# Moving the wait for the output store from in front of a block's closing barrier to behind it

## The chip, the cores and the metric

The kernel runs on one core of one Trainium2 chip. The metric is device time in microseconds (us). A core has five engines with an instruction stream each: TensorE (PE), VectorE (DVE), ScalarE (ACT), GpSimd (POOL) and SyncE (SP, which here issues nearly all DMAs). In this program they meet through semaphores: counters that an engine or a DMA adds to and that another engine waits on.

Everything here happens in the last four microseconds of a 658 us program.

## The reference

One decode step: layer norm of one token, grouped-query attention over a cache of 65,536 keys (32 query heads, 8 key-value heads of 128), the output projection, a GELU feed-forward beside it, and the residual.

```python
xn = _layernorm(x)
# A: q = xn @ wq; scores = q k^T / sqrt(128); p = softmax(scores); o = p v; o @ wo
# B: gelu(xn @ w1 + b1) @ w2 + b2
return x + A(xn, k_cache, v_cache, wq, wo) + B(xn, w1, b1, w2, b2)   # (1, 1, 512), bf16
```

## The kernel before

A small scheduler records each engine's operations with the semaphore waits that they need, and they are then emitted, engine by engine, inside one block. The end of the kernel is the only part that the change touches:

```python
# ... the last matmuls of the output projection write pR on PE ...
sch.op(DVE, lambda: dve.tensor_copy(out=fin_bf[0:NR, :], in_=pR[0:NR, 0:128]),      # L820
       reads=[f"pss{R}"], writes=["fin"])
ev_out = sch.dma(                                                                    # L824
    SP,
    lambda: sp.dma_start(out=out[0, 0].rearrange("(kt p) -> kt p", p=128), in_=fin_bf[0:NR:32, :]),
    sem_out, reads=["fin"], writes=["out_dram"],
)
sch.wait_ev(SP, ev_out)        # SyncE waits until the 1 KB result has landed

with nc.Block() as block:                                                            # L829
    # ... one function for each engine emits that engine's recorded operations ...
    @block.sync
    def _(e):
        _emit(e, SP.ops)
    # ...
# nothing follows
```

A block ends in a barrier of all engines. In the program as built it is this (shortened; every engine first branches into this common piece, and its Drain is the instruction with which it reports to the barrier):

```
ACT, PE, DVE, SP:  Drain, adds 1 to "gather";  then wait for "release", take 1 off it
POOL:              Drain;  wait until gather is 4, take 4 off;  add 4 to "release"
```

## Time and profile before

| | before |
|---|---|
| median time | 658.44 us (6 runs, 658.15 to 658.76) |
| span of the kernel's own instructions | 656.5 us |
| from the store's issue to its landing | 1.64 us |
| from the landing to the kernel's last instruction | 0.39 us |

First the page of the kernel before: its DMA row over 40 slices of the span (tenths of busy time), the load queue, and the chain that ended last.

```profile
DMA  8999999999999999999999999999999999999997
...
q1 hardware_dynamic: 8616, 280.50, 99.2%
...
DMA 63%; PE 34%; issue 2%; DVE 0%; SPq 0%
```

The kernel is a stream of the caches through the DMA engines; nothing in the change can touch that. So the reader has to look at the tail. These are three lines of the waits view of the kernel before, for SyncE's queue: source line, releaser, then total, count and longest wait in us.

```profile
SPq L824 <- DVE fin_bf L820: 16.6, 1, 16.6
SPq L829 <- DMA out_dram<-fin_bf: 1.0, 1, 1.0
SPq L829 <- PEq L829: 0.2, 1, 0.2
```

SyncE waits for VectorE's last copy, issues the store, then waits 1.0 us for the landing, and only then reaches the barrier, where it waits 0.2 us more. Now the instructions of line L829, the closing barrier of the kernel before. These are eight of the view's eleven lines, put in order of start; left out are SyncE, ACT and DVE passing at 656.5. Each line gives engine and operation, count, duration in ns (least, median, most), and the start in us.

```profile
L829 ACTq DRAIN  x1: 746/746/746, 643.0 to 643.0; - x1
L829 POOLq DRAIN  x1: 164/164/164, 643.9 to 643.9; - x1
L829 PEldq DRAIN  x1: 425/425/425, 653.8 to 653.8; - x1
L829 DVEq DRAIN  x1: 330/330/330, 654.2 to 654.2; - x1
L829 SPq COMPARE_BRANCH  x1: 33/33/33, 656.2 to 656.2; - x1
L829 SPq DRAIN  x1: 7/7/7, 656.3 to 656.3; - x1
L829 POOLq EVENT_SEMAPHORE  x2: 17/17/17, 656.4 to 656.4; - x2
L829 PEldq EVENT_SEMAPHORE  x1: 51/51/51, 656.5 to 656.5; - x1
```

Four engines have drained by 654.5 and then stand still for two microseconds. SyncE, held by its wait for the store (the wait sits on its branch), comes last, at 656.3.

The span ends with the kernel's own last instruction, but the program does not. The trace also records every semaphore update, and in these records activity goes on for 1.9 us behind the span. No view of the profile prints them; they are read from the packed trace. The Trainium skill, "Runtime: NRT & Kernel Launch", section "The ~15µs preamble/postamble breakdown", says what this is: behind the kernel the runtime puts a barrier over all engines, then a reset of the user semaphores, then another barrier. For the runtime's barrier in front of a kernel it describes a serpentine over the five engines in eight hops. It reserves semaphore 2 for that barrier (section "Semaphores 0–2 are reserved"). The records agree (nine updates make eight hops); in us from the store's issue, for the kernel before:

```
landing 1.64 | barrier released 1.95 | kernel's last instruction ends 2.03
semaphore 2, first pass : 2.264 2.298 2.505 2.549 2.572 2.677 2.716 2.751 2.797
other semaphores reset  : up to 3.36
semaphore 2, second pass: nine more updates, the last at 3.941
```

I call the first nine updates the closing chain, and the time from the store's issue to the last update of semaphore 2 the *tail*. It is 3.94 us before. That last update stands 658.46 us behind the start of the span, close to the time measured (658.33 us in the profiled run).

### The profile page before, as it was taken

To read this page: it belongs to the slowest core of one execution; us is meant where nothing else is said; L and a number is where in the kernel's file an instruction comes from. 1 tells how busy PE (TensorE), PEld (TensorE's weight loads), DVE (VectorE), ACT (ScalarE), POOL (GpSimd) and SP (SyncE) were. 2 spreads that over 40 slices of the span, in tenths; PEclk is the share of its full clock that TensorE was granted. 3 is DMA by queue.
4 is the path that set the end of the run, shared out by engine and by line. 5 is a ranking of instruction groups with operands and counts; after the bars stand their busy time and mean duration, and the time that the engine had idled before them with its cause. 6 is when DMAs were issued, how large, how long until landed. Compare 5 with 4: busy or idle time off the path is not lost.

```text
span 656.5 us, 27968 instructions
## 1 busy us (share of the span) xinstructions
PE 539.3 (82%) x12682; PEld 512.1 (78%) x12682; DVE 275.7 (42%) x574; ACT 244.9 (37%) x454; POOL 2.9 (0%) x27
## 2 busy tenths in 40 slices
PE   2388699999789797878969787896978879797897
PEld 0187698988689697868969786896968779686896
DVE  3244162635435172442616245171634516254353
ACT  0134153534425152351605335161443516144251
POOL 0000000000000000000000000000000000000000
PEclk9788597878759596885959778596877859687595
DMA  8999999999999999999999999999999999999997
GB/s 369 438 436 426 429 430 433 439 425 461 401 441 439 421 453 413 437 427 445 433 417 449 417 445 421 427 457 411 447 419 447 429 419 441 423 459 408 431 433 295
DMA packets 8774, 280.65 MB, mean 427 GB/s; under 512 B 1082, under 2 KB 1596, under 8 KB 1724
## 3 DMA queue, kind: packets, MB, share of 16 engines
q1 hardware_dynamic: 8616, 280.50, 99.2%
q8 instruction: 8, 0.13, 0.1%
q10 hardware_dynamic: 148, 0.01, 0.0%
q14 instruction: 2, 0.02, 0.0%
HBM read 280.50 MB, written 0.00 MB: 427 GB/s over the span
## 4 chain that ended last, share of the span: by engine, by line
DMA 63%; PE 34%; issue 2%; DVE 0%; SPq 0%
DMA kv<-in_A_k_cache_dram 61%; PE pst L590 27%; PE pss L610 4%; DMA kv<-in_A_wo_dram 3%; PE pO L681 2%; PE pA L637 0%; PE pA L648 0%; DVE pmax L618 0%; PE pA L697 0%; PE pss L805 0%; DVE gmax L639 0%; DVE diag L641 0%; SPq L470 0%; SPq L467 0%; SPq L463 0%
## 5 line engine op out<-in xcount | busy, mean ns | idle before, releaser
L590 PE MATMUL pst<-ident_bf,kv 128*128 128x128 bf16 x4096 | 284.3, 236 | 34.0 <-DMA kv<-in_A_k_cache_dram 33.9
L600 ACT ACTIVATE kt_ring<-pst 128x1024 bf16<-128x1024 bf16 x192 | 195.6, 1027 | 312.1 <-PE pst L590 310.7
L590 PEld LDWEIGHTS pst<-ident_bf,kv 128*128 128x128 bf16 x4096 | 266.0, 107 | 42.4 <-DMA kv<-in_A_k_cache_dram 35.5
L598 DVE COPY kt_ring<-pst 128x1024 bf16<-128x1024 bf16 x320 | 210.7, 687 | 121.1 <-PE pst L590 118.7
L681 PE MATMUL pO<-P_bf,kv 128*128 128x4 bf16 x4096 | 115.1, 166 | 37.1 <-DMA kv<-in_A_v_cache_dram 32.1
L681 PEld LDWEIGHTS pO<-P_bf,kv 128*128 128x128 bf16 x4096 | 113.6, 104 | 38.5 <-DMA kv<-in_A_v_cache_dram 33.1
L610 PE MATMUL pss<-q_cur,kt_ring 128*128 128x4 bf16 x4096 | 111.9, 164 | 4.9 <-issue 4.9
L610 PEld LDWEIGHTS pss<-q_cur,kt_ring 128*128 128x128 bf16 x4096 | 109.3, 96 | 5.1 <-issue 5.1
L659 ACT ACTIVATE P_bf<-pss,negm 128x128 bf16<-128x128 f32 x128 | 50.9, 547 | 67.6 <-DVE negm L651 67.6
L690 DVE COPY o_all<-pO 128x4 f32 (+1 forms) x32 | 5.2, 161 | 120.3 <-PE pO L681 119.5
L618 DVE TENSOR_REDUCE pmax<-pss 128x4 f32<-128x512 f32 x32 | 22.1, 691 | 68.8 <-PE pss L610 68.8
L659 ACT ACTIVATION_READ_ACCUMULATOR P_bf<-pss,negm 128x1 f32 x128 | 35.3, 276 | 0.0
L648 PEld LDWEIGHTS pA<-diag,ones_f 4*128 4x128 f32 x64 | 12.6, 245 | 17.8 <-DVE diag L641 16.2
L637 PE MATMUL pA<-ident_f,pmax 128*4 128x128 f32 x64 | 14.0, 305 | 12.5 <-DVE pmax L618 12.5
L648 PE MATMUL pA<-diag,ones_f 4*128 4x4 f32 x64 | 15.4, 309 | 10.0 <-DVE diag L641 10.0
L637 PEld LDWEIGHTS pA<-ident_f,pmax 128*4 128x4 f32 x64 | 2.9, 84 | 15.7 <-DVE pmax L618 14.0
L639 DVE TENSOR_REDUCE gmax<-pA 4x1 f32<-4x128 f32 x32 | 8.8, 274 | 9.1 <-PE pA L637 9.1
L673 DVE COPY sums_all<-sums 128x8 f32 (+1 forms) x16 | 2.7, 171 | 23.4 <-ACT P_bf L659 23.4
L697 PE MATMUL pA<-sums_all,ones_f 128*128 128x128 f32 x32 | 12.4, 491 | 0.0
L651 DVE TENSOR_SCALAR negm<-pA 128x4 f32<-128x4 f32 x32 | 5.1, 161 | 10.8 <-PE pA L648 10.8
L697 PEld LDWEIGHTS pA<-sums_all,ones_f 128*128 128x128 f32 x32 | 8.1, 312 | 0.0
L641 DVE TENSOR_SCALAR diag<-ident_f,gmax 4x4 f32<-4x4 f32 x32 | 7.0, 218 | 1.1
(78 smaller groups left out, 49.5 us busy)
## 6 DMA issues: line engine op xcount, KB each, us to landing
kv<-in_A_k_cache_dram SPq DMA_DIRECT2D x32, 4096.0 KB, 27.5
kv<-in_A_v_cache_dram SPq DMA_DIRECT2D x4, 4096.0 KB, 23.2
kv<-in_A_wq_dram SPq DMA_DIRECT2D x1, 4096.0 KB, 12.2
kv<-in_B_w_dram SPq DMA_DIRECT2D x2, 1792.0 KB, 18.0
kv<-in_A_wo_dram SPq DMA_DIRECT2D x1, 2048.0 KB, 23.0
kv<-in_A_wo_dram SPq DMA_DIRECT2D x1, 1024.0 KB, 25.1
kv<-in_A_wo_dram SPq DMA_DIRECT2D x1, 512.0 KB, 25.9
kv<-in_A_wo_dram SPq DMA_DIRECT2D x1, 384.0 KB, 16.4
```

What stands on the lines that cost most here:

```text
L590: lambda tb=tb, at=at, b=b, tt=s * TPB + t: pe.transpose(pst[tb][:, at * 128:(at + 1) * 128], slot[b][:, tt, :], ident_bf[:, :]),
L598: e, fn = DVE, lambda tb=tb, dst=dst: dve.tensor_copy(out=dst, in_=pst[tb][:, :])
L600: e, fn = ACT, lambda tb=tb, dst=dst: act.activation(out=dst, in_=pst[tb][:, :], func=ACTF.Copy)
L610: lambda k=k, kb=kb, at=at, t=t: pe.matmul(pss[k][:, at:at + HPG], lhsT=kt_ring[:, kb * BCOL + t * 128:kb * BCOL + (t + 1) * 128], rhs=q_c ...
L618: lambda k=k: dve.tensor_reduce(out=pmax[:, :], in_=pss[k][:, 0:CW].rearrange("p (t j) -> p j t", j=HPG), axis=AX.X, op=ALU.max),
L637: sch.op(PE, lambda: pe.matmul(pA[0:HPG, PA_ST:PA_ST + 128], lhsT=pmax[:, 0:HPG], rhs=ident_f[:, :], start=True, stop=True), reads=["pmax" ...
L639: sch.op(DVE, lambda: dve.tensor_reduce(out=gmax4[:, :], in_=pA[0:HPG, PA_ST:PA_ST + 128], axis=AX.X, op=ALU.max), reads=["pA"], writes=[" ...
L641: sch.op(DVE, lambda: dve.tensor_scalar(out=diag4[:, :], in0=ident_f[0:HPG, 0:HPG], scalar1=gmax4[0:HPG, 0:1], scalar2=None, op0=ALU.mult) ...
L648: sch.op(PE, lambda: pe.matmul(pA[:, PA_SB:PA_SB + HPG], lhsT=ones_f[0:HPG, 0:128], rhs=diag4[0:HPG, 0:HPG], start=True, stop=True), reads ...
L659: lambda k=k, at=at, j=j, src=src: act.activation(out=P_v[k][:, :, j], in_=src[:, :, j], func=ACTF.Exp, bias=negm[:, at:at + 1], scale=1.0 ...
L681: lambda k=k, t=t: pe.matmul(pO[:, 0:HPG], lhsT=vslot[:, k * TPD + t, :], rhs=P_v[k][:, t, :], start=t == 0, stop=t == TPD - 1),
L697: sch.op(PE, lambda: pe.matmul(pA[:, PA_SUM:PA_SUM + NC], lhsT=ones_f[:, :], rhs=sums_all[:, :], start=True, stop=True), reads=["ones_f", ...
```

## The change

SyncE still waits for the store, but as its own last instruction, behind the barrier. The output has still landed before the program ends, because the runtime's closing barrier needs SyncE too (experiments 2 and 4 show it waiting for SyncE).

```diff
         sem_out, reads=["fin"], writes=["out_dram"],
     )
-    sch.wait_ev(SP, ev_out)
 
     with nc.Block() as block:
@@
         @block.tensor
         def _(e):
             _emit_rolled(e, PE.ops, marks)
+
+    sp.wait_ge(ev_out.sem, ev_out.val)
```

The intent is that the engines pass the barrier while the store is still on its way.

## The prediction

> **What bounds the kernel now.** It streams the key and value caches. The page's slices show the 16 DMA engines busy at nine tenths in 38 of 40 slices, the load queue at 99.2% of the span, 427 GB/s; the chain that ended last is 63% DMA and 34% PE. The span is 656.5 us, the timed median 658.46 us. The change touches none of that: the instruction order of PE, DVE, ACT and POOL is the same in both programs, and SyncE differs only behind the output store.
>
> **The tail of before** (trace records at the end of the span; the waits view of SyncE's queue agrees: 1.0, 0.2 us):
> - 654.52: the store is issued, 0.63 us, until 655.15.
> - 656.15: its semaphore is full. SyncE waits 1.0 us for it in its branch (starts 656.17, 33 ns).
> - 656.33: SyncE's drain, 0.12 us after the branch, the last arrival at the barrier. The others drained earlier: PE 653.8, DVE 654.2, ACT and POOL near 643 to 644.
> - 656.36 and 656.44: POOL gathers and releases; 656.48 to 656.49: four engines pass; PE ends last at 656.54.
>
> So branch, drain, gather and release cost 656.54 - 656.15 = 0.39 us in series behind the landing.
>
> **What the change does.** It moves that stretch into the shadow of the landing. SyncE branches at about 655.15 and drains by 655.35, the engines pass near 655.5, and SyncE alone waits for the landing, about 0.6 us more. It adds one SyncE wait (17 to 33 ns). It removes no transfer and not the landing time. The Trainium skill, "DMA: Bandwidth & Descriptors", section on the anatomy of one DMA, puts about 2 us of fixed cost on a transfer, mostly the write receipt; here issue to landing is 656.15 - 654.52 = 1.63 us, packets moving at 655.75 to 655.81. That stays, because SyncE must still end behind it.
>
> **Behind the span.** The Trainium skill, "Runtime: NRT & Kernel Launch", launch sequence, says a closing barrier over all engines and semaphore resets follow the kernel. The trace agrees: updates of semaphore 2 run from 656.78 to 657.31 in one chain, resets of the others to 657.88, a second chain from 658.10 to 658.46. In the first chain the third step came 0.21 us after the second, in the second chain 0.04 us: an engine arrived late. Now SyncE alone will be late. If it stands first in that chain, the 0.17 us hole goes too; if later, it is its own gain only. I can't tell which.
>
> **Sum** (estimate). Span: 656.54 to about 656.19, -0.35 us. Timed: -0.32 to -0.5 us, say -0.4 us. All of it is on the critical path, being the end of the program, but it is 0.06% of the time, and the three runs of before spread over 0.6 us (658.15 to 658.76).
>
> **Predicted: 658.05 us, range 657.6 to 658.5.** Faster by over 2%: 0.003; within 2%: 0.994; slower: 0.003.
>
> **What would show each step.**
> - Right: barrier events of ACT, DVE, PE, POOL near 655.4 to 655.6, before the store's landing; the span's last instruction is SyncE's wait, 20 to 50 ns after the landing; span about 0.35 us shorter measured from the store's issue; issue to landing still 1.5 to 1.8 us; the first chain of semaphore 2 begins sooner after the landing, or waits in the middle for SyncE.
> - Wrong: the barrier finishing behind the landing; a longer issue to landing; the closing chain no sooner.
>
> **What would make it wrong.** Run noise is as large as the effect, so the median may move either way. SyncE's drain may wait for the outstanding store: then nothing is hidden. The landing time may vary by some tenths. The timed interval may begin or end elsewhere than I read it.

## The result, and the profile after

The changed kernel takes 657.60 us (median of 6 runs, 657.51 to 657.80) against 658.44 us (658.15 to 658.76). The ratio is 0.9988, with a 95% interval of 0.9975 to 1.0001. Ratios here are the mean time of one kernel's runs over that of the other's of the same rounds, so they are not quite the ratio of the medians. The interval just includes 1. Yet over the whole study the 16 runs of the changed kernel lie between 657.48 and 658.03 us and 33 runs of the kernel before between 658.14 and 658.76 us, so they don't overlap. The means of the three sessions differ by 0.78, 0.68 and 0.76 us. The sign of the gain is not in doubt.

The page after, for the same three lines:

```profile
DMA  8999999999999999999999999999999999999997
...
q1 hardware_dynamic: 8616, 280.50, 99.3%
...
DMA 64%; PE 34%; issue 2%; DVE 0%; SPq 0%
```

The body is the same, as it should be. SyncE's waits after the change:

```profile
SPq L824 <- DVE fin_bf L820: 17.7, 1, 17.7
...
SPq L850 <- DMA out_dram<-fin_bf: 0.4, 1, 0.4
SPq L828 <- PEq L828: 0.2, 1, 0.2
```

The wait for the landing has moved from the barrier's line to a line of its own, L850, and is 0.4 us, where it was 1.0. The other 0.6 us now passes while SyncE drains and goes through the barrier. The barrier after, which is now L828 (seven of ten lines; left out are SyncE, ACT and DVE passing at 655.8):

```profile
L828 POOLq EVENT_SEMAPHORE  x2: 17/17/17, 655.7 to 655.8; - x2
L828 ACTq DRAIN  x1: 751/751/751, 642.2 to 642.2; - x1
L828 POOLq DRAIN  x1: 166/166/166, 644.0 to 644.0; - x1
L828 PEldq DRAIN  x1: 285/285/285, 654.0 to 654.0; - x1
L828 DVEq DRAIN  x1: 328/328/328, 654.2 to 654.2; - x1
L828 SPq DRAIN  x1: 417/417/417, 655.2 to 655.2; - x1
L828 PEldq EVENT_SEMAPHORE  x1: 51/51/51, 655.8 to 655.8; - x1
```

And the new last instruction of the span, from the view of line L850:

```profile
L850 SPq EVENT_SEMAPHORE  x1: 17/17/17, 656.2 to 656.2; - x1
```

Two things are to be seen. The barrier passes at 655.8, ahead of the landing at 656.2, as intended. And SyncE's drain, 7 ns before, is 417 ns now that it comes right behind the store's issue, so it still holds the barrier up.

The semaphore records of the two profiled runs, in us from the store's issue:

| | before | after | difference |
|---|---|---|---|
| store landed | 1.636 | 1.640 | +0.00 |
| barrier released | 1.946 | 1.241 | -0.705 |
| kernel's last instruction ends | 2.025 | 1.674 | -0.35 |
| closing chain, 1st update | 2.264 | 1.560 | -0.704 |
| closing chain, 3rd update | 2.505 | 1.800 | -0.705 |
| closing chain, 9th update | 2.797 | 2.093 | -0.704 |
| last update of semaphore 2 (tail) | 3.941 | 3.236 | -0.705 |

The span, measured from the store, shrank by the 0.35 us that I had predicted. The program shrank by twice that. Every event behind the kernel moved by 0.705 us, and that is what the *release of the barrier* moved by, not what SyncE's last instruction moved by. From release to the last update it is 1.995 us in both. That gives the question for the experiments.

### The profile page after: what moved, and what is told of

Same layout as the page of the kernel before. It is cut to its first block, busy times and chain, and to the rows that moved or that the text cites. A ratio compares the mean times of both kernels' runs of the same rounds, so it can differ in the third digit from the quotient of the medians.

```text
span 656.2 us, 27968 instructions
## 1 busy us (share of the span) xinstructions
PE 536.5 (82%) x12682; PEld 509.5 (78%) x12682; DVE 275.3 (42%) x574; ACT 244.9 (37%) x454; POOL 2.9 (0%) x27
## 4 chain that ended last, share of the span: by engine, by line
DMA 64%; PE 34%; issue 2%; DVE 0%; SPq 0%
DMA kv<-in_A_k_cache_dram 61%; PE pst L590 27%; PE pss L610 4%; DMA kv<-in_A_wo_dram 3%; PE pO L681 2%; PE pA L637 0%; PE pA L648 0%; DVE pmax L618 0%; PE pA L697 0%; DVE gmax L639 0%; PE pss L805 0%; DVE diag L641 0%; SPq L470 0%; SPq L467 0%; SPq L463 0%
```

## The experiments

**Theory "release".** The end of the program follows the release of the kernel's own barrier. SyncE's wait for the landing hides behind something else that the closing chain waits for.

**Rival "landing".** The end follows SyncE's wait for the landing, as the prediction had it, and the equal 0.705 us are a coincidence.

**Rival "layout".** One more instruction and a shifted program gave the gain, not the order.

All experiments start from the changed kernel, not from the kernel before. All results were correct.

### 1. Both waits

```diff
+    sch.wait_ev(SP, ev_out)
+
     with nc.Block() as block:
```

> The changed kernel with the old wait in front of the barrier put back, the new one behind it kept. Tail = from the store's issue to the last update of semaphore 2: 3.94 us in the kernel before, 3.24 us in the changed one. If the place of the wait gave the gain (0.7 us in the tail, 0.8 us in the time), this is the kernel before again: tail 3.9 to 4.0 us, time 658.3 to 658.5 us. If the other length or layout of the program gave it, the tail stays near 3.2 us and the time near 657.6 us.

Measured: 658.34 us against 658.30 us of the kernel before (5 and 9 runs), ratio 0.9999 (0.9986 to 1.0013); tail 3.948 us. From the waits view of this run:

```profile
SPq L830 <- DMA out_dram<-fin_bf: 1.0, 1, 1.0
...
SPq L830 <- PEq L830: 0.2, 1, 0.2
```

With the old wait back in front, the kernel before is back, though the new wait still stands behind the barrier. "Layout" falls. The place of the wait makes the gain.

### 2. SyncE late behind the landing

Each pair costs SyncE a signal to itself and a wait for it.

```diff
     sp.wait_ge(ev_out.sem, ev_out.val)
+    lag = nc.alloc_semaphore("lag")
+    for n in range(12):
+        sp.sem_inc(lag, 1)
+        sp.wait_ge(lag, n + 1)
```

> The changed kernel with SyncE held up behind its wait for the store by twelve waits for its own signal (estimate 0.6 to 0.9 us in all; the trace gives the real lag). Theory landing: the end follows SyncE's last wait, so the whole lag is added to tail and time. Theory release: the end follows the barrier's release and SyncE has slack, so tail and time grow by the lag less the slack, which would show as a hole in the closing chain of semaphore 2 at SyncE's place in it; a slack of 0.1 to 0.5 us.

Measured: 658.51 us (658.14 to 658.54) against 658.30 us; tail 3.954 us. SyncE's last event stands 2.487 us behind the store's issue, in the changed kernel 1.657 us, so the lag was 0.83 us. The tail grew by 0.72 us. So about 0.11 us were absorbed, and the rest counted in full. The closing chain shows where: its 4th update came at 1.855 us (1.845 us in the changed kernel), its 5th at 2.646 us, which is 0.159 us behind SyncE's last event. SyncE is the fifth and innermost in the chain. The 5th update moved by 0.778 us, so 0.05 us of the lag was absorbed at SyncE's own place; another 0.06 us went at the next step, which took 0.043 us where it had taken 0.105 us. So SyncE was nearly, but not quite, what the end waited for. On the lag alone "release" and "landing" both give about this, and they differ only by the 0.11 us; the next run tells them apart.

### 3. The release late

```diff
+    spare = sb("spare", [128, 512], F32)
+    for _ in range(3):
+        sch.op(DVE, lambda: dve.memset(spare[:, :], 0.0), writes=["spare"])
     ev_out = sch.dma(
```

> The changed kernel with three memsets (about 0.49 us each) on VectorE behind the last copy, so that VectorE is last at the barrier: the release moves from 1.24 us behind the store's issue to about 1.6 us, still ahead of the landing at about 1.64 us. Theory landing: tail stays 3.24 us and time 657.6 us. Theory release: both grow by as much as the release moves, 0.3 to 0.4 us, that is a tail of about 3.6 us and 658.0 us, and the last update of semaphore 2 stays 2.0 us behind the release.

Measured: 658.36 us (658.31 to 658.46) against 658.30 us, tail 4.103 us. The experiment overshot its mark. I had reckoned with 0.49 us for a memset, but each waits for the one before and they start 0.66 us apart, so VectorE drained later than planned. From the view of the barrier's line in this run:

```profile
L831 POOLq EVENT_SEMAPHORE  x2: 17/17/17, 656.4 to 656.5; - x2
...
L831 SPq DRAIN  x1: 417/417/417, 655.2 to 655.2; - x1
L831 DVEq DRAIN  x1: 661/661/661, 655.7 to 655.7; - x1
```

The release came 2.018 us behind the issue, with the landing, at 1.642 us, already past. If the end followed the landing, the tail would have stayed at 3.24 us. If it followed SyncE's last event (2.112 us here, 0.455 us later than in the changed kernel), it would have been 3.69 us. It was 4.10 us: the release moved by 0.777 us and the first nine updates moved by 0.777 us with it (the 9th from 2.093 to 2.870 us). "Landing" falls for this regime. The remaining 0.09 us lie between the two passes of semaphore 2. The same 0.09 us turned up in one later profile of the unaltered changed kernel (tail 3.333 us), so that stretch varies by itself.

### 4. The store behind the barrier too

```diff
+    n_sp = len(SP.ops)
     ev_out = sch.dma(
@@
         def _(e):
-            _emit(e, SP.ops)
+            _emit(e, SP.ops[:n_sp])
@@
+    _emit(sp, SP.ops[n_sp:])
     sp.wait_ge(ev_out.sem, ev_out.val)
```

> The changed kernel with the store itself issued behind the barrier too: the release no longer waits for SyncE's drain (0.42 us), and comes about 0.3 us behind the end of VectorE's last copy, at the cost of a later issue and landing. From the end of that copy the changed kernel takes 3.26 us to the last update of semaphore 2. Theory release alone: about 2.3 us, 0.9 us less time. Theory landing (landing + 1.60 us): issue 0.25 us later, so 3.5 us, and time 657.8 to 657.9 us. If the end is the later of the two, it is the second, less SyncE's slack.

Measured: 657.64 us (657.60 to 657.89) against 658.30 us. From the end of VectorE's copy to the last update it is 3.400 us, where the changed kernel has 3.263 us. First two lines of the waits view of this run, then two of the view of its barrier:

```profile
SPq L829 <- PEq L829: 17.4, 1, 17.4
...
SPq L852 <- DMA out_dram<-fin_bf: 1.0, 1, 1.0
```

```profile
L829 POOLq EVENT_SEMAPHORE  x2: 17/17/17, 654.4 to 654.5; - x2
L829 SPq DRAIN  x1: 122/122/122, 637.1 to 637.1; - x1
```

Now the barrier is released 1.3 us earlier in relation to the store than in the changed kernel, and the first four updates of the closing chain are all done 0.51 us behind the store's issue. Then the chain stands still for 1.3 us, until SyncE has its landing (1.649 us), and its 5th update comes 0.159 us behind the landing, at 1.808 us (0.142 us behind SyncE's last event). In this regime the end follows the landing. From the issue the tail is 3.116 us, 0.12 us less than in the changed kernel: that is SyncE's slack there, the same 0.11 us that run 2 gave. But the store itself was issued 0.26 us later behind the copy, so nothing is won. "Release alone" had promised 2.3 us, and falls too.

So neither theory alone is right. The closing chain waits for the later of two things: an engine that needs long behind the release, and SyncE's landing. Before the change, SyncE's landing sat in front of the release, so the two were added. After it they run side by side, and they are nearly equal.

### 5. Which engine is it?

The same twelve self-signals, put behind the barrier on one of the other engines instead of on SyncE.

```diff
+    lag = nc.alloc_semaphore("lag")
+    for n in range(12):
+        pe.sem_inc(lag, 1)        # or act, pool, dve
+        pe.wait_ge(lag, n + 1)
```

> The changed kernel with PE, not SyncE, held up behind the barrier by twelve waits for its own signal. Which engine makes the third step of the closing chain come 0.56 us behind the release? If PE, the hole opens at the third step and grows by the whole lag. If another, the hole opens elsewhere or the lag is partly absorbed.

> The same lag on ScalarE (ACT): if it sets the third step, that step moves by the whole lag; otherwise another step shows the hole (the first, if ScalarE begins the chain), or part of the lag is absorbed.

> The same lag on GpSimd (POOL): if it sets the third step, that step moves by the whole lag; otherwise another step shows the hole, or part of the lag is absorbed.

> The same lag on VectorE: if VectorE sets the third step, that step moves by the whole lag; otherwise another step shows the hole, or part of the lag is absorbed.

Measured, one look each, from the traces (us; the "hole" is the long gap that opens in the closing chain; "lag" is how much later the engine's last event stands behind the store's issue than in the changed kernel, "tail" is measured against 3.236 us):

| engine held up | lag | hole opens at update | from its last event to that update | tail grew by | absorbed |
|---|---|---|---|---|---|
| PE | 1.956 | 1st | 0.347 | 1.845 | 0.11 |
| ACT | 1.037 | 2nd | 0.146 | 0.687 | 0.35 |
| POOL | 1.227 | 3rd | 0.554 | 1.437 | none |
| DVE | 1.434 | 4th | 0.182 | 1.037 | 0.40 |
| SyncE (run 2) | 0.83 | 5th | 0.159 | 0.718 | 0.11 |

The chain goes PE, ACT, POOL, DVE, SyncE and back. POOL is the one that makes its 3rd update come 0.56 us behind the release: it takes 0.55 us from its last own event to its place in the chain, the longest of the five, and it is the only one whose lag is not absorbed in the tail. Its 3rd update moved by 1.197 of the 1.227 us of lag, so POOL had at most 0.03 us to spare. PE, the first that the expectations name, is not the one. Two things agree. From the release to the 3rd update it is 0.559 us in the kernel before, in the changed kernel and in runs 3 and 4, wherever the release lay. And where PE or ACT held the chain up for longer than POOL needs, the step from the 2nd to the 3rd update took 0.039 us and not 0.206 us. Each engine was held up in one profile only. That POOL's lag even cost 0.21 us more than itself comes from a second hole, at POOL's place on the way back (the 7th update 0.285 us behind the 6th, normally 0.039 us). Why POOL needs so long, and why twice in that run, the traces don't show.

### 6. The barrier earlier still

If the landing can be made the only thing left, 0.11 us should be had by taking the barrier out of the tail altogether. PE waits for the last weights anyway around 652.5 us, so the barrier was put there: the last matmuls, the last copy, the store and its wait all stand behind it.

```diff
     for i, (g0, n) in enumerate(WP):
+        n_pe = len(PE.ops)                 # the last group's first matmul
@@
     NR = 32 * (KT - 1) + 1
+    n_dve, n_sp = len(DVE.ops), len(SP.ops)
@@  (inside the block: SP.ops[:n_sp], DVE.ops[:n_dve], PE.ops[:n_pe])
+    _emit(pe, PE.ops[n_pe:])
+    _emit(dve, DVE.ops[n_dve:])
+    _emit(sp, SP.ops[n_sp:])
     sp.wait_ge(ev_out.sem, ev_out.val)
```

It ran beside the changed kernel, twice, in two sessions.

> The changed kernel once more, beside the next one on the same chip: time 0.6 to 0.9 us under the kernel before, tail (store's issue to last update of semaphore 2) 3.24 us, its landing hidden by 0.14 us.

> The closing barrier moved further ahead: the last 32 matmuls of the output projection, VectorE's last copy, the store and its wait all stand behind it, so PE, VectorE and SyncE meet where PE waits for weights anyway, and the store is issued at once behind the copy. If the end is the later of release + 2.0 us and SyncE's last wait + about 1.45 us (0.14 us of that being SyncE's way into the chain), only the second is left: tail 3.1 us, that is 0.1 to 0.15 us less than the changed kernel, as long as PE loses nothing at the barrier. If the barrier costs PE time (drain, release, restart), VectorE's copy comes later against the landing of the last weights, and the time is that of the changed kernel or worse by up to 0.5 us.

> A repeat, for the one run of five at 658.64 us: if it is chance, five runs near 657.5 us; if the early barrier has a second ending, about one in five again 1 us longer at an unchanged span. Tail 3.12 us.

> The changed kernel beside it: 657.6 to 657.7 us, tail 3.24 us; the early barrier should be 0.1 us under it, which five runs with a scatter of 0.2 us can hardly tell.

Lines of the barrier's view of the first of these runs, with the last line of that view's list of who waited for it:

```profile
L830 POOLq EVENT_SEMAPHORE  x2: 17/17/17, 652.3 to 652.4; - x2
L830 SPq DRAIN  x1: 122/122/122, 637.6 to 637.6; - x1
...
L830 PEldq DRAIN  x1: 945/945/945, 651.3 to 651.3; - x1
...
  PE pss L805: 0.3, 1
```

The barrier passes at 652.4 us at the cost of 0.3 us of PE's waiting, in a stretch where PE waits for weights before and after. The tail was 3.120 and 3.123 us, 0.12 us under the changed kernel's 3.236 us (3.245 us and, with the wandering 0.09 us, 3.333 us in the other two profiles). The chain of the first of these runs also waits where run 5 puts the engines: PE's last matmuls stand behind the barrier now and the 1st update is late (0.175 us ahead of the issue, 1.886 us behind the release), the 4th comes 0.145 us behind VectorE's copy, and the 5th waits for SyncE. With the release so early, POOL's step is 0.038 us. So the mechanism holds in the trace. In the time it does not show: 657.62 us against 657.67 us in the first session, 657.64 us against 657.52 us in the second. One run of the ten took 658.64 us with an unchanged span of 656.1 us, so its extra microsecond lay behind the span; it did not come again in five more runs, and its cause is open. I do not count this version as faster than the changed kernel.

## Why the prediction was right or wrong

The forecast, 658.05 us with a range of 657.6 to 658.5, holds the measured 657.60 us only at its lower edge. The size was off: 0.4 us forecast, 0.7 to 0.8 us measured. The range had been drawn wide for run noise. The sum's own largest gain, 0.5 us off 658.46 us, ends at 657.96 us and misses the measured time, so that the range held is partly luck.

- *"What bounds the kernel now"*: right. The DMA row and the chain did not change.
- *The tail of before, 0.39 us in series behind the landing*: right as far as the span goes. The span's tail shrank by 0.35 us, as forecast.
- *"SyncE branches at about 655.15 and drains by 655.35, the engines pass near 655.5"*: wrong by 0.3 us. The drain took 417 ns and the engines passed at 655.8. I had named a drain that waits for the store as a danger; it was far longer than the 7 ns of before, but it did not wait for the landing, which came 0.53 us behind its end.
- *"SyncE must still end behind" the landing*: right (1.640 us from issue to landing; SyncE's last event 0.017 us behind it).
- *"Sum: timed -0.32 to -0.5 us"*: this is the step that failed. It took SyncE for the engine that the closing chain would wait for, so that the gain would be what SyncE's last instruction moves, plus a 0.17 us hole if SyncE stood first. The runs showed that SyncE stands fifth, with 0.11 to 0.12 us to spare, and that the chain waits for POOL, which needs 0.55 us from its last own event to its update. POOL's clock starts at the release, and the release moved by 0.705 us. The term that was mis-sized is that one: 0.7 us and not 0.3 to 0.5 us.
- The 0.17 us hole that I saw at the 3rd update was POOL. It is there in both kernels, unchanged (0.207 and 0.206 us from the 2nd update to the 3rd). I had read it as a late engine, rightly, and left open whether it would go with the change. It stayed.
- *"Run noise is as large as the effect"*: too cautious. The effect was 0.7 us, and the runs of the two kernels never overlapped.

## What to carry to other kernels

Where the end of the program waits for an engine anyway, as runs 2 and 4 show it here for SyncE, a wait that only this engine needs belongs behind the closing barrier, on that engine: in front of it, the landing and everyone's way out are added; behind it, they overlap. The end of a profile's span is not the end of the program, so a change in the tail should be followed in the semaphore records until they fall silent, and each event compared by what it moved *with*. Once two paths run side by side, what remains to be won on either is only their difference: here 0.12 us, which the time no longer shows.

## What the Trainium skill lacked or had wrong

- "Runtime: NRT & Kernel Launch", breakdown table: it gives about 1.5 us for the closing barrier, 1.5 us for the reset of semaphores, and 2 us for a second barrier and the DMA rings. Here the first pass takes 0.53 us (2.264 to 2.797 us), 0.77 us counted from the kernel's last instruction, and everything from that instruction to the last update 1.92 us before and 1.56 us after. Work that updates no semaphore is not in these records, so the sums need not cover the same things. That a barrier passes to and fro over five engines is right: nine updates. The page's 355 ns for eight hops, 44 ns each, fits the second pass, where nobody is late: 0.357 us (3.584 to 3.941 us). As a mean only: the single hops take 23 to 98 ns.
- The text of the same page lacks the order in the closing barrier (PE, ACT, POOL, DVE, SyncE and back) and the time that each engine takes from its last own event to its place: 0.35, 0.15, 0.55, 0.18 and 0.16 us when that engine is the late one (SyncE 0.14 us in runs 4 and 6). These decide how late each engine may be.
- "Perfetto Trace Analysis", section "Sequencer-only Instruction (DRAIN, etc)", lists a drain as sequencer work without more. SyncE's drain took 7 ns with its store landed, 417 ns right behind the issue of the four-row output store, and 122 ns behind the 128-row weight loads (runs 4 and 6). It ended 0.10 us behind the first of five updates of the store's semaphore and 0.53 us ahead of the landing. "DMA: Bandwidth & Descriptors", section "Why a DMA increments its semaphore by 16 and not by 1", says that for a transfer on fewer than 16 engines the sequencer writes the missing increments itself, at once. The one early update and four later ones agree with that, but the early one came 1.01 us behind the issue. That the drain waits for this write fits the numbers and was not tested.
- The same DMA page's 2 us of fixed cost for a transfer was 1.64 to 1.66 us in all profiles here, with the packets of the store moving 1.2 to 1.3 us behind its issue. The page gives its figure for DMAs issued from GpSimd, which the prediction did not say; this store was issued from SyncE. So this is an addition and not a contradiction.
